# The opening of a linear-attention and state-space block: k of chunks 0 and 1 interleaved by passes, the first loads in four other parts

## The chip, the cores and the metric

The kernel runs on one core of a Trainium2 chip. The metric is the device time of one execution in microseconds (us), lower is better. Before the change the median of three runs is 179.42 us (178.81 to 181.05).

The engines are named as in the profile: PE is TensorE, which multiplies matrices, and PEld its weight loads; DVE is VectorE, ACT is ScalarE, POOL is GpSimd, SP is SyncE, which here issues all DMA transfers. Each engine works through its own queue in order and waits for the others by semaphores.

## The reference

One block mixes two branches of the same input x (2048 x 448):

```
qkv  = x @ wqkv                      # 448 -> 3 x 448, 16 heads of 28
phi  = lambda t: where(t > 0, t + 1, exp(t)) + 1e-6
kv   = sum over s of phi(k)[s] outer v[s], per head;   z = sum over s of phi(k)[s]
a    = (phi(q) @ kv / (phi(q) . z + 1e-6)) @ wo          # linear attention, not causal
b    = irfft(rfft(x) * rfft(K)) + x * D_skip             # long convolution, K from the state-space parameters
g    = sigmoid(sum(x * gate_w))
out  = g * a + (1 - g) * b
```

All is in 32-bit floats, and the kernel must keep that accuracy.

## The kernel before

**Tiling.** The 2048 rows of x are 16 chunks of 128 (`NC`). The width 448 is contracted in four blocks (`J`): three of 128 and block 0, which holds the last 64 columns. Each x chunk comes twice from memory: turned (`turned[c]`, 128 x 512, the four blocks side by side, used as weights of TensorE) and plain (`plain[c]`).

**Two halves of each number.** TensorE multiplies in the type fp32r, which keeps fewer bits. So each operand is split: the high half is a copy into fp32r (done by ScalarE, or VectorE), the low half is the original minus the high half (`low`, line 228). A product is then three: high x high, low x high and high x low. In `pieces` (line 307) these are the lists `hh`, `lh` and `hl`, one entry per block. Block 0 has only 64 columns; its other 64 rows hold the same x again against the low half of the weights, so `hl` lacks block 0, and a projection of one chunk is **eleven** matmuls (4 + 4 + 3) into one PSUM tile. I write h1 for the product of high halves of block 1, l1 for x low by weights high, w1 for x high by weights low; where loads, copies and low halves are spoken of, w1 is the weight block 1 itself.

**The order is written out by hand.** The scheduling is manual: every engine's queue has its instructions in the order of the program, and only the waits are put in by the framework. So the order of the lines from 419 on is the order of each queue.

**The opening** (lines 180 to 252 and 419 to 460):

- Before the data are there, `fill(WARM)` (line 252) issues nine bf16 matmuls of a tile of ones into a PSUM tile that nobody reads.
- SP issues the first loads in the three parts of `PARTS` (lines 30 and 200 to 209): part 1 is x of chunk 0 and block 1 of the k weights (256 + 224 KB), part 2 is weight blocks 2 and 3 (448 KB), part 3 weight block 0 and x of chunk 1 (224 + 256 KB). Behind them come two transfers of 512 KB (x of chunk 2 turned, and the plain x of chunks 0 to 2), the q weights (two of 450 KB), the skip row (224 KB) and x of chunk 3 (line 219, `load_x`).
- VectorE copies the high half of chunk 0's x in two pieces (420, 422), and subtracts the low halves of x and of each weight block (423 to 426); ScalarE copies the high halves of the weight blocks 1, 2, 3, 0 (421 and 256).
- `pieces(0, ..., "k", "w")` (427) orders the eleven products of chunk 0 as h1 l1 h2 l2 w1 h3 l3 w2 w3 h0 l0; they are issued in groups with three more filling matmuls between (428 to 430).
- `split_t(1)` (432) copies chunk 1's x to its high half on ScalarE and subtracts the low half on POOL; then `project(1, ...)` issues chunk 1's k, all eleven in a row, into the PSUM tile `v0`. Chunk 2 follows in the same way into `v1`.
- `k_feature`, `k_high` and `k_low` (346 to 361) make phi(k): two passes on ScalarE, one on VectorE, then `pkh` on ScalarE and `pkl` on VectorE. `zb` sums phi(k) on VectorE. `split_n(c)` splits plain x into `xn`: high on ScalarE, low on POOL.
- `do_g(c)` (384) adds x^T phi(k) of the chunk to four PSUM tiles that stay for the whole kernel: eleven matmuls, of which the first takes `pkh`, the second `pkl`, the third the low half of `xn`.
- The q weights are split (`split_w(..., wqh, ...)`, 445 to 448), and `project(0, wqh, ...)` (452) makes q of chunk 0, with block 0 last.

After that the 16 chunks go through q, k, the state update and the skip branch in a steady order until about 119 us; then the accumulated state is turned into small matrices, and the last 16 rounds (`attend`) make the output.

Of the kernel before, what the change touches and what calls it, by code (L numbers as in the profile page):

```python
# [8 lines left out]
F32R = mybir.dt.float32r  # L9
# [6 lines left out]
P = 128  # L16
S = 2048
D = 448
# [6 lines left out]
NAT = 4 * P  # L25
LO = NAT + D
XC = LO + 64
NX = XC - NAT + D
WARM = 9
PARTS = ((("x", 0), ("w", 1)), (("w", 2), ("w", 3)), (("w", 0), ("x", 1)))  # L30
FIRST = 2 * NAT + J * D
QA = 1
QW = D + 16
# [100 lines left out]
def gated_mix_kernel(ctx: ExitStack, tc: tile.TileContext, xin, wq_d, wvo_d, abc_d, ldt_d, dsk_d,  # L134
                     turn_d, cst_d, first_d, gin_d, lag_d, out):
    nc = tc.nc
    PE, ACT, DVE, POOL, SP = nc.tensor, nc.scalar, nc.vector, nc.gpsimd, nc.sync
# [15 lines left out]
    wkh, wkl = wk2[:, 0], wk2[:, 1]  # L153
# [21 lines left out]
    xt_p = work.enter_context(tc.tile_pool(name="xt", bufs=4))  # L175
# [11 lines left out]
    xt, xn, turned, plain = {}, {}, {}, {}  # L187
# [11 lines left out]
    o = 0  # L199
    for part in PARTS:  # L200
        e = o
# [7 lines left out]
        o = e  # L209
# [17 lines left out]
    def low(eng, o, r, h):  # L227
        eng.tensor_tensor(out=o, in0=r, in1=h.bitcast(F32), op=ALU.subtract)  # L228

    def split_t(c):  # L230
        w = xt[c] = xt_p.tile([P, 2 * NAT], F32R, name="xt", tag="t")
        ACT.copy(w[:, :NAT], turned[c])  # L232
        low(POOL, w[:, NAT:], turned[c], w[:, :NAT])

    def split_n(c):
        r, w = plain[c], xn_p.tile([P, NX], F32R, name="xn", tag="n")
        xn[c] = w
        ACT.copy(w[:, :XC - NAT], r)  # L238
        low(POOL, w[:, XC - NAT:], r[:, :D], w[:, :D])
        if c > 2:  # L240
            skip(c)

    def skip(c):
        POOL.tensor_tensor(out=y[:, c], in0=plain[c][:, :D], in1=dsk, op=ALU.mult)  # L244
# [3 lines left out]
    def fill(n):  # L248
        for _ in range(n):
            PE.matmul(idle, lhsT=warm[:, :P], rhs=warm, start=True, stop=True)  # L250

    fill(WARM)
    ACT.activation(oks, warm[:DJ, :1], AF.Exp)

    def split_w(j, h, l, w, eng):
        ACT.copy(h[:, j], w[j] if isinstance(w, dict) else w[:, j])
        low_w(j, h, l, w, eng)

    def low_w(j, h, l, w, eng):
        r = slice(0 if j else 64, P)  # L260
        w = w[j] if isinstance(w, dict) else w[:, j]
        low(eng, (l if j else h)[r, j], w[r], h[r, j])
# [44 lines left out]
    def pieces(c, wh, wl, n, tag, last=None):  # L307
        o = ps.tile([P, 512], F32, name=tag, tag=tag)
        h, l = ([xt[c][:, i + k * P:i + (k + 1) * P] for k in range(J)] for i in (0, NAT))
        hh, lh, hl = ([(a[k], w[:, k]) for k in range(J)] for a, w in ((h, wh), (l, wh), (h, wl)))  # L310
        hl = hl[1:]
        if last == "x":
            seq = hh + hl + lh
        else:
            seq = [p for k in range(J) for p in (hh[k], lh[k])] + hl
            if last == "w":
                seq = seq[2:6] + seq[8:9] + seq[6:8] + seq[9:] + seq[:2]

        def run(count):
            for _ in range(min(count, len(seq))):  # L320
                a, b = seq.pop(0)
                run.n += 1
                PE.matmul(o[:, :n], lhsT=a, rhs=b, start=run.n == 1, stop=not seq)  # L323
        run.n = 0
        return o, run

    def project(*args, **kw):
        o, run = pieces(*args, **kw)
        run(11)
        return o  # L330
# [15 lines left out]
    def k_feature(c, o):  # L346
        e = tp.tile([P, D], F32, name="e", tag="e")
        pks[c] = o[:, :D]
        ACT.activation(e, pks[c], AF.Relu, scale=-1.0)  # L349
        ACT.activation(e, e, AF.Exp, scale=-1.0)  # L350
        DVE.scalar_tensor_tensor(out=pks[c], in0=pks[c], scalar=1.0, in1=e, op0=ALU.add, op1=ALU.max)  # L351

    def k_high(c):
        pkh[c] = tp.tile([P, D], F32R, name="pkh", tag="pkh")
        ACT.add(pkh[c], pks[c], 1e-6)

    def k_low(c):
        pk = pks.pop(c)
        pkl[c] = tp.tile([P, D], F32R, name="pkl", tag="pkl")
        for o, a, op in ((pkl[c], pkh[c].bitcast(F32), ALU.subtract), (zb, zb, ALU.add))[::-1 if c == NC - 1 else 1]:  # L360
            DVE.scalar_tensor_tensor(out=o, in0=pk, scalar=1e-6, in1=a, op0=ALU.add, op1=op)
# [54 lines left out]
        for _ in range(n):  # L416
            next(prep, None)

    w = xt[0] = xt_p.tile([P, 2 * NAT], F32R, name="xt", tag="t")
    DVE.tensor_copy(w[:, P:NAT], turned[0][:, P:])  # L420
    ACT.copy(wkh[:, 1], wkr[1])  # L421
    DVE.tensor_copy(w[:, :P], turned[0][:, :P])
    low(DVE, w[:, NAT:], turned[0], w[:, :NAT])
    low_w(1, wkh, wkl, wkr, DVE)
    for j in (2, 3, 0):
        split_w(j, wkh, wkl, wkr, DVE)
    ko, run = pieces(0, wkh, wkl, D, "k", "w")
    for n, f in ((1, 1), (1, 1), (6, 0), (1, 1), (2, 0)):
        run(n)
        fill(f)  # L430
    ko = [ko]
    split_t(1)
    ko.append(project(1, wkh, wkl, D, "v0", "x"))
    split_t(2)
    ko.append(project(2, wkh, wkl, D, "v1", "x"))
    k_feature(0, ko[0])
    k_high(0)
    split_n(0)
    k_low(0)
    k_feature(1, ko[1])  # L440
    split_n(1)
# [20 lines left out]
    for c in range(2, NC - 2):  # L462
# [7 lines left out]
        ko = project(c + 1, wkh, wkl, D, "v1" if c in (2, 4) else "k")  # L470
# [39 lines left out]
        for j in {11: (0, 1), 12: (2, 3)}.get(c, ()):  # L510
            w = xn_p.tile([P, NX], F32R, name="wo", tag="n")[:DJ, :2 * D].rearrange("p (i d) -> p i d", i=2)
# [113 lines left out]
    c = NC - 2  # L625
    POOL.memset(rows[DT:RX, D:2 * D], 0.0)
    gate(0, c)
    ko = project(c + 1, wkh, wkl, D, "k")
# [31 lines left out]
    gates_c(NC - 2, g[0], "pkl")()  # L660
    norm_b(1)
    qo, q_run = pieces(c + 1, wqh, wql, D + 2, "q")
    for i in range(5):
        phi(i)
# [170 lines left out]
def _layout(inputs):  # L835
# [15 lines left out]
    def tiles(w):  # L851
        o = np.zeros((P, J, w.shape[1]), np.float32)
        for k in range(3):
            o[:, k + 1] = w[k * P:(k + 1) * P]
        o[:64, 0] = w[384:]
        o[64:, 0] = w[384:]
        return o
# [8 lines left out]
                          for n in ("B_log_A_real", "B_A_imag", "B_C_real", "B_C_imag")]  # L866
                         + [np.repeat(np.asarray(inputs["B_log_dt"]).reshape(D, 1, 1), P, axis=1),
                            x[:, ::-1].transpose(2, 1, 0)], axis=2)
    wk = tiles(w[:, D:2 * D])
    first = np.concatenate([wk[:, i] if kind == "w" else xin[i, :, :NAT] for part in PARTS for kind, i in part]  # L870
                           + [xin[2, :, :NAT], xin[0, :, NAT:], xin[1, :, NAT:], xin[2, :, NAT:]], axis=1)
# [42 lines left out]
```

## Time and profile before

| | us |
|---|---|
| median of three runs | 179.42 |
| lowest and highest run | 178.81, 181.05 |
| the profiled execution | 178.89 |
| its span in the trace | 177.1 |
| PE busy | 170.5 |
| ACT busy | 96.2 |
| DVE busy | 113.4 |
| POOL busy | 121.1 |

The profile is of one execution. Its span runs from the first to the last recorded instruction; 1.79 us lie around it. Rows of the timeline read: start, length, engine, line of the kernel, operation, output <- inputs, shape, count, and in brackets how long the engine stood idle before and what ended that. A row with a count over 1 covers several instructions in a row, from the first start to the last end. Rows of the chain that ended last read: start, length, engine, tile and line.

### The profile page before, as it was taken

The page shows a single profiled execution, that of the slowest core. Times are in us where ns is not written, and L with a number is a line of the kernel's source. Part 1 is how long each engine was busy: PE and PEld are TensorE (multiplying, and loading weights), DVE is VectorE, ACT ScalarE, POOL GpSimd, SP SyncE. Part 2 cuts the span into 40 slices and gives each one's busy share as a digit, 9 for nine tenths or more (in the row PEclk, how much of TensorE's full clock was granted, in tenths as well). Part 3 has the DMA queues.
Part 4 walks back from the last instruction along what each step waited for, and adds up shares of the span by engine and source line. Part 5 has one row for each costly group of instructions (what it writes and reads, how often), then busy time and mean ns, then how long its engine had stood idle before and what let it go on. Part 6 is the DMA issues. An engine that isn't in the chain of part 4 may idle for free.

```text
span 177.1 us, 2803 instructions
## 1 busy us (share of the span) xinstructions
PE 170.5 (96%) x876; PEld 151.6 (86%) x876; DVE 113.4 (64%) x244; ACT 96.2 (54%) x220; POOL 121.1 (68%) x128
## 2 busy tenths in 40 slices
PE   6999999999999999999999999999889999999991
PEld 2699999999999999999989999988678999999991
DVE  1747538698857274462824619376999988977451
ACT  3789388874536244272435753464645555564541
POOL 5167476977349969688599999439089999893100
PEclk9999999999999999999999999999999999999999
DMA  5999973095003303032133000000121212222313
GB/s 174 414 316 269 249 223 127 8 418 227 4 1 120 106 16 119 5 120 75 45 121 123 0 0 1 0 2 5 21 47 52 105 74 86 104 75 82 111 55 104
DMA packets 7963, 18.61 MB, mean 105 GB/s; under 512 B 2045, under 2 KB 4810, under 8 KB 7818
## 3 DMA queue, kind: packets, MB, share of 16 engines
q1 hardware_dynamic: 7946, 18.41, 31.6%
q8 instruction: 7, 0.11, 0.3%
q14 instruction: 10, 0.08, 0.2%
HBM read 14.38 MB, written 3.67 MB: 102 GB/s over the span
## 4 chain that ended last, share of the span: by engine, by line
PE 91%; DVE 4%; DMA 2%; ACT 1%; issue 0%; DVEq 0%; ACTq 0%
PE a L612 21%; PE g L392 20%; PE q L323 18%; PE k L323 16%; PE v L323 6%; PE tr L587 3%; DMA y<-in 2%; PE v L400 2%; PE v L399 2%; PE k L706 1%; DVE kvl L228 1%; DVE wk L694 1%; PE m L686 0%; DVE rc L677 0%; PE q L250 0%; DVE den L530 0%
## 5 line engine op out<-in xcount | busy, mean ns | idle before, releaser
L612 PE MATMUL a<-wk,th 128*128 128x448 f32 (+1 forms) x170 | 36.9, 363 | 0.7 <-DVE wk L694 0.7
L392 PE MATMUL g<-pkh,xn 128*128 128x448 f32 x112 | 35.6, 366 | 0.0
L612 PEld LDWEIGHTS a<-wk,th 128*128 128x128 f32 x170 | 29.5, 189 | 2.9 <-DVE wk L694 0.9
L323 PE MATMUL k<-wk,xt 128*128 128x448 f32 x132 | 29.6, 368 | 0.2 <-ACT wk L421 0.2
L351 DVE SCALAR_TENSOR_TENSOR k<-k,e 128x448 f32<-128x448 f32 x12 | 7.6, 632 | 32.1 <-ACT e L350 32.1
L323 PE MATMUL q<-wqh,xt 128*128 128x450 f32 x120 | 28.0, 370 | 0.0
L323 PEld LDWEIGHTS k<-wk,xt 128*128 128x128 f32 x132 | 24.6, 188 | 3.1 <-ACT wk L421 0.7
L412 POOL TENSOR_TENSOR y<-y,t 128x448 f32<-128x448 f32 x16 | 18.8, 1175 | 12.3 <-DVE t L404 11.9
L228 POOL TENSOR_TENSOR xn<-xr,xn 128x448 fp32r<-128x448 f32 x16 | 19.3, 1203 | 9.2 <-ACT xn L238 9.0
L323 PEld LDWEIGHTS q<-wqh,xt 128*128 128x128 f32 x120 | 22.5, 189 | 2.2 <-issue 0.2
L392 PE MATMUL g<-pkl,xn 128*128 128x448 f32 x64 | 23.4, 366 | 0.0
L392 PEld LDWEIGHTS g<-pkh,xn 128*128 128x128 f32 x112 | 21.0, 188 | 2.5
L349 ACT ACTIVATE e<-k 128x448 f32<-128x448 f32 x12 | 6.5, 546 | 28.0 <-PE k L323 27.9
L525 POOL TENSOR_TENSOR prod<-pq,zb 128x448 f32<-128x448 f32 x16 | 18.4, 1159 | 4.3 <-ACT zb L647 3.1
L244 POOL TENSOR_TENSOR y<-xr,rows 128x448 f32<-128x448 f32 x16 | 18.9, 1184 | 0.0
L228 POOL TENSOR_TENSOR xt<-xr,xt 128x512 fp32r<-128x512 f32 x14 | 18.2, 1299 | 0.4 <-ACT xt L232 0.4
L550 POOL TENSOR_TENSOR pn<-pq,den 128x336 f32<-128x336 f32 x16 | 12.1, 754 | 8.3 <-DVE den L539 4.4
L617 DVE SCALAR_TENSOR_TENSOR ot<-y,og,a 128x448 f32<-128x448 f32 (+1 forms) x17 | 10.6, 626 | 5.6 <-PE a L612 5.5
L595 DVE TENSOR_TENSOR th<-tr,th 128x512 fp32r<-128x512 f32 x16 | 11.0, 690 | 3.0 <-ACT th L594 2.5
L594 ACT CAST th<-tr 128x512 fp32r<-128x512 f32 x16 | 9.4, 590 | 5.5 <-PE tr L587 5.3
L392 PEld LDWEIGHTS g<-pkl,xn 128*128 128x128 f32 x64 | 11.2, 175 | 1.0
L323 PE MATMUL q<-wql,xt 128*128 128x450 f32 x45 | 11.7, 364 | 0.0
(149 smaller groups left out, 301.6 us busy)
## 6 DMA issues: line engine op xcount, KB each, us to landing
xr<-in SPq DMA_DIRECT2D x15, 512.0 KB, 6.0
out<-ot SPq DMA_DIRECT2D x15, 224.0 KB, 2.0
pq<-in SPq DMA_DIRECT2D x4, 448.0 KB
wvo<-in SPq DMA_DIRECT2D x1, 1792.0 KB
y<-in SPq DMA_DIRECT2D x2, 480.0 KB
y<-in SPq DMA_DIRECT2D x2, 450.0 KB
u<-t SPq DMA_DIRECT2D x30, 1.8 KB, 1.8
y<-in SPq DMA_DIRECT2D x1, 448.0 KB, 4.4
```

The source lines that it names most:

```text
L228: eng.tensor_tensor(out=o, in0=r, in1=h.bitcast(F32), op=ALU.subtract)
L244: POOL.tensor_tensor(out=y[:, c], in0=plain[c][:, :D], in1=dsk, op=ALU.mult)
L323: PE.matmul(o[:, :n], lhsT=a, rhs=b, start=run.n == 1, stop=not seq)
L351: DVE.scalar_tensor_tensor(out=pks[c], in0=pks[c], scalar=1.0, in1=e, op0=ALU.add, op1=ALU.max)
L392: PE.matmul(g[i][:a.shape[1], :D], lhsT=a, rhs=b, start=c == 0 and n == 0, stop=c == NC - 1 and n == len(seq) - 1)
L412: POOL.tensor_tensor(out=y[:, c], in0=y[:, c], in1=t, op=ALU.add)
L525: POOL.tensor_tensor(out=pd[c], in0=pq[:, c], in1=zb, op=ALU.mult)
L550: POOL.tensor_tensor(out=n[:, :3, :DJ].rearrange("p j (h d) -> p j h d", h=4), in0=a, in1=r[:, :H - 4].rearrange("p (j h) -> p j h", j=3)[ ...
L594: ACT.copy(h, ov)
L595: DVE.tensor_tensor(out=l, in0=ov, in1=h.bitcast(F32), op=ALU.subtract)
L612: PE.matmul(a[:, lo:hi], lhsT=u_, rhs=w_[:, lo:hi], start=n == 0, stop=n == 10)
L617: DVE.scalar_tensor_tensor(out=ot[:, lo:hi], in0=y[:, c, lo:hi], scalar=og[:, c:c + 1], in1=a[:, lo:hi], op0=ALU.mult, op1=ALU.add)
```

## The change

Three things change in the opening, and nothing behind `k_low(0)`.

1. The first loads come in four parts: x of chunks 0 and 1 (512 KB), weight block 1 (224 KB), weight blocks 2 and 3 (448 KB), weight block 0 (224 KB). The same bytes, one transfer more.
2. The 22 products of k of chunks 0 and 1 are interleaved in an order written out as a string per chunk. The three filling matmuls between them go; one is added ahead (`WARM` 10). In order, with c0 and c1 for the chunks: c0 h1, c1 h1, c0 l1, c0 w1, c1 w1, c0 h2, c1 h2, c0 l2, c0 h3, c1 l1, c1 h3, c0 w2, c0 l3, c0 w3, c1 l2, c1 w2, c1 l3, c0 h0, c0 l0, c1 w3, c1 h0, c1 l0.
3. The high half of chunk 1's x is copied by ScalarE ahead of weight block 1, and its low half is subtracted by VectorE, behind the low half of weight block 1, instead of by POOL. `split_n(0)` stands ahead of `k_high(0)` instead of behind it.

```diff
-WARM = 9
-PARTS = ((("x", 0), ("w", 1)), (("w", 2), ("w", 3)), (("w", 0), ("x", 1)))
+WARM = 10
+PARTS = ((("x", 0), ("x", 1)), (("w", 1),), (("w", 2), ("w", 3)), (("w", 0),))
...
-            if last == "w":
+            if last and len(last) > 1:
+                seq = [{"h": hh, "l": lh, "w": [None] + hl}[i[0]][int(i[1])] for i in last.split()]
+            elif last == "w":
                 seq = seq[2:6] + seq[8:9] + seq[6:8] + seq[9:] + seq[:2]
...
-    w = xt[0] = xt_p.tile([P, 2 * NAT], F32R, name="xt", tag="t")
+    w, w1 = (xt_p.tile([P, 2 * NAT], F32R, name="xt", tag="t") for _ in range(2))
+    xt[0], xt[1] = w, w1
     DVE.tensor_copy(w[:, P:NAT], turned[0][:, P:])
+    ACT.copy(w1[:, :NAT], turned[1])
+    DVE.tensor_copy(w[:, :P], turned[0][:, :P])
     ACT.copy(wkh[:, 1], wkr[1])
-    DVE.tensor_copy(w[:, :P], turned[0][:, :P])
     low(DVE, w[:, NAT:], turned[0], w[:, :NAT])
     low_w(1, wkh, wkl, wkr, DVE)
+    low(DVE, w1[:, NAT:], turned[1], w1[:, :NAT])
     for j in (2, 3, 0):
         split_w(j, wkh, wkl, wkr, DVE)
-    ko, run = pieces(0, wkh, wkl, D, "k", "w")
-    for n, f in ((1, 1), (1, 1), (6, 0), (1, 1), (2, 0)):
-        run(n)
-        fill(f)
-    ko = [ko]
-    split_t(1)
-    ko.append(project(1, wkh, wkl, D, "v0", "x"))
+    ko, runs = zip(*(pieces(c, wkh, wkl, D, t, o) for c, t, o in (
+        (0, "k", "h1 l1 w1 h2 l2 h3 w2 l3 w3 h0 l0"), (1, "v0", "h1 w1 h2 l1 h3 l2 w2 l3 w3 h0 l0"))))
+    for c, n in ((0, 1), (1, 1), (0, 2), (1, 1), (0, 1), (1, 1), (0, 2), (1, 2), (0, 3), (1, 3), (0, 2), (1, 3)):
+        runs[c](n)
+    ko = list(ko)
     split_t(2)
     ko.append(project(2, wkh, wkl, D, "v1", "x"))
     k_feature(0, ko[0])
+    split_n(0)
     k_high(0)
-    split_n(0)
     k_low(0)
```

## The prediction

> **What bounds the kernel now.** I read the page first (share of each engine), then the chain that ended last, then the rows of the first 20 us engine by engine, because the change touches nothing later than the first output of chunk 1.
>
> ```profile
> span 177.1 us, 2803 instructions
> PE 170.5 (96%) x876; PEld 151.6 (86%) x876; DVE 113.4 (64%) x244; ACT 96.2 (54%) x220; POOL 121.1 (68%) x128
> ```
>
> TensorE is busy nearly all the time, so time is gained only where it stands still, or lost where a new wait makes it stand still. The profiled execution took 178.89 us, 1.79 us more than its span, and lies 0.53 us under the median of 179.42 us.
>
> ```profile
> 0.76 3.81 DMA y<-in
> 4.59 0.57 ACT wk L421
> 5.21 0.47 PE k L323
> 5.91 0.43 PE k L323
> 6.57 1.43 PE k L323 x7
> 8.23 0.59 PE k L323 x2
> 8.82 4.48 PE v L323 x22
> 13.30 4.46 PE g L392 x22
> ```
>
> Columns: start, length, what. The opening is a load (to 4.59), a copy on ScalarE, and then matmuls. One matmul of the dense stretch takes 4.48/22 = 0.204 us. The eleven of chunk 0's k come in four pieces with gaps; the 22 of chunks 1 and 2 (`v`) and the 22 of both first state updates (`g`) come without.
>
> ```profile
> 13.13 0.37 PE L392 MATMUL g<-pkh,xn 128*128 128x448 f32 x1
> 13.34 0.36 PE L392 MATMUL g<-pkl,xn 128*128 128x448 f32 x1
> 15.57 0.36 PE L392 MATMUL g<-pkl,xn 128*128 128x448 f32 x1
> 17.59 0.99 PE L323 MATMUL q<-wqh,xt 128*128 128x450 f32 x4
> ```
>
> From the first matmul (5.21) to the first of the state update (13.13) pass 7.92 us; 33 matmuls at 0.204 need 6.72. So **1.20 us** is all that dense interleaving can win there. After 17.6 only the shift counts: the chain of waits shows TensorE dense behind it.
>
> **The first matmul moves back.** Today the first part carries x of chunk 0 and w1 (480 KB), the second w2 and w3 (448), the third w0 and x of chunk 1 (480).
>
> ```profile
> 0.76 1.35 SPq L208 DMA_DIRECT2D y<-in  x3
> 4.59 0.56 ACT L421 CAST wk<-y 128x448 fp32r<-128x448 f32 x1 [2.34 <-DMA y<-in]
> 5.67 0.57 ACT L256 CAST wk<-y 128x448 fp32r<-128x448 f32 x1 [0.52 <-DMA y<-in]
> 6.87 0.57 ACT L256 CAST wk<-y 128x448 fp32r<-128x448 f32 x1 [0.16 <-DMA y<-in]
> 4.68 0.53 SPq L192 DMA_DIRECT2D xr<-in  x1
> ```
>
> ScalarE waits for each part and starts at 4.59, 5.67 and 6.87, that is after 480, 928 and 1408 KB: 415 and 400 KB per us, with no fixed cost between parts. On this line the new parts come at 4.67 (both x, 512 KB), 5.21 (w1, 736 KB), 6.31 (w2 and w3, 1184 KB), 6.87 (w0, 1408 KB). A fourth issue costs SP 1.35/3 = 0.45 us, still over by 2.6, long before its data are due. SP's later loads move by one place: the ninth issue (4.68 today, just as the first part is in) becomes the tenth and goes out at about 5.2, but the transfers ahead of it (1408 KB of parts, two of 512 KB, 900 KB of q weights, 224 KB) take more than 8 us at that rate, so the queue is full beyond 11 us and nothing lands later for it.
>
> w1's landing is not in this trace. It lies between 4.67 (together with x) and 5.67 (the start after 928 KB); I take 5.21, by bytes. The Trainium skill, "DMA: Bandwidth & Descriptors", section on the anatomy of one DMA, gives each transfer a fixed 2.0 us besides its bytes, measured on the software path: read as a cost per part in sequence, that would put w1 about 2 us later, and the sum at some 2 us slower. The 1.08 us from the first to the second part contradict it for queued transfers: the fixed part overlaps.
>
> On ScalarE the high half of chunk 1's x now stands first.
>
> ```profile
> 11.16 0.61 ACT L238 CAST xn<-xr 128x512 fp32r<-128x512 f32 x1
> 11.67 0.55 ACT L349 ACTIVATE e<-v 128x448 f32<-128x448 f32 x1
> ```
>
> A 512-wide copy blocks ScalarE for 0.51 us, so it runs from 4.67 and frees the engine at 5.18: w1's copy then waits for its load and ends at 5.21 + 0.56 = 5.77; the first matmul follows 0.06 later, as now (4.59 + 0.56 to 5.21), at **5.83**, 0.62 us later than before. The copies of w2, w3, w0 end at 6.87, 7.35 and 7.82.
>
> **VectorE's queue** has one 512-wide subtraction more (POOL has it now, with time to spare).
>
> ```profile
> 4.59 0.36 DVE L420 CAST xt<-y 128x384 fp32r<-128x384 f32 x1 [3.17 <-DMA y<-in]
> 4.87 0.22 DVE L422 CAST xt<-y 128x128 fp32r<-128x128 f32 x1
> 5.12 0.69 DVE L228 TENSOR_TENSOR xt<-y,xt 128x512 fp32r<-128x512 f32 x1
> 5.73 0.62 DVE L228 TENSOR_TENSOR wk<-y,wk 128x448 fp32r<-128x448 f32 x1
> 6.27 0.63 DVE L228 TENSOR_TENSOR wk<-y,wk 128x448 fp32r<-128x448 f32 x1
> ```
>
> Spacing is 0.61 us behind a 512-wide one and 0.54 behind a 448-wide one. So chunk 0's low half ends at 5.89, w1's at 6.43, chunk 1's at 7.04 (0.61 of delay for those behind it), w2's at 7.58, w3's at 8.12, w0's at 8.67.
>
> **The 22 interleaved matmuls**, each at the later of 0.204 behind the last one and 0.06 behind its operand. c0 h1 5.83, c1 h1 6.03, c0 l1 6.24; c0 w1 waits for w1's low half, 6.49 instead of 6.44; c1 w1 6.69; c0 h2 waits for w2's copy, 6.93 instead of 6.90; then c1 h2, c0 l2 at 7.13 and 7.34. From there nothing is late: h3 stands at 7.54 (copy 7.35), c1 l1 at 7.74 (7.04), c0 w2 at 8.15 (7.58), c0 w3 at 8.56 (8.12), c0 h0 at 9.37 (8.67). The last of chunk 0 (the nineteenth) starts at 9.57, the last of chunk 1 at 10.18, chunk 2's k at 10.39, and the state update could start at **12.63**, 0.50 before today's 13.13. So 1.20 us of gaps become 0.08, and 0.62 is paid for the later start.
>
> **What is late next.** k of chunk 0 is finished later, though k of chunk 1 is earlier than it need be.
>
> ```profile
> 8.86 0.55 ACT L349 ACTIVATE e<-k 128x448 f32<-128x448 f32 x1
> 9.44 0.58 ACT L350 ACTIVATE e<-e 128x448 f32<-128x448 f32 x1
> 10.05 0.63 DVE L351 SCALAR_TENSOR_TENSOR k<-k,e 128x448 f32<-128x448 f32 x1 [1.96 <-ACT e L350]
> 10.72 0.55 ACT L355 ACTIVATE pkh<-k 128x448 fp32r<-128x448 f32 x1 [0.70 <-DVE k L351]
> 11.30 0.62 DVE L361 SCALAR_TENSOR_TENSOR pkl<-k,pkh 128x448 fp32r<-128x448 f32 x1 [0.61 <-ACT pkh L355]
> 11.84 0.62 DVE L361 SCALAR_TENSOR_TENSOR zb<-k,zb 128x448 f32<-128x448 f32 x1
> 11.85 1.16 POOL L228 TENSOR_TENSOR xn<-xr,xn 128x448 fp32r<-128x448 f32 x1 [1.27 <-ACT xn L238]
> ```
>
> This serial chain from the end of k to `pkl` takes 11.92 - 8.86 = 3.06 us. Today it ends 1.4 us before its use at 13.34. After the change k ends at 9.57 + 0.37 = 9.94, the chain starts at 9.99, `pkh` is there at 12.41 and `pkl` at 13.05. The state update's first matmul goes at 12.63, but its second must wait to **13.11** where TensorE would be ready at 12.83: 0.28 us lost, a new wait. The moved `split_n(0)` costs nothing: the copy of xn now runs in ScalarE's 0.70 us of idling before `pkh` and POOL's low half ends at about 12.9, before its use at 13.31; with the old order it would end at about 14.1.
>
> Chunk 1: ScalarE starts its relu 0.44 behind `pkh` of chunk 0 (10.72 to 11.16), 12.30; exp 12.88 to 13.46; VectorE is free of `zb` at 13.52; its max ends at 14.15, `pkh` at 14.73, `pkl` at 15.39. Its matmul, 2.23 behind that of chunk 0 as today (13.34 to 15.57), would go at 15.34 and waits to **15.45**: 0.12 us before 15.57. Behind ScalarE's delayed `pkh` (some 0.65 us) are the four copies of the q weights.
>
> ```profile
> 15.49 1.49 ACT L256 CAST wqh<-y 128x450 fp32r<-128x450 f32 x3
> 16.59 1.02 POOL L228 TENSOR_TENSOR wql<-y,wqh 128x450 fp32r<-128x450 f32 x1 [1.00 <-ACT wqh L256]
> 17.01 1.08 DVE L228 TENSOR_TENSOR wqh<-y,wqh 64x450 fp32r<-64x450 f32 x1 [0.24 <-ACT wqh L256]
> ```
>
> All shift by about 0.65: w0's last row ends at 18.75. The q projection, at 17.59 - 0.12 = 17.47, takes the w0 products last, from 9 x 0.204 behind, 19.31. It is covered with 0.55 us to spare; past that, each us of delay would cost a us. Chunk 2's feature and chunk 3's x are used from 22 us on.
>
> **Sum**: +0.62 (start) - 1.12 (gaps) + 0.28 (`pkl` of chunk 0) + 0.11 (of chunk 1), about -0.1 us. Against its own execution that is 178.8, against the median 179.42 - 0.1 = **179.3 us**. The three fills left out cost nothing if the clock holds.
>
> **Rivals.**
>
> *TensorE goes back to the slow clock (slower).*
>
> ```profile
> PEclk9999999999999999999999999999999999999999
> 1.48 3.55 PE L250 MATMUL q<-warm 128*128 128x512 bf16 x9 [1.48 <-DVE warm L181]
> 4.01 0.15 PEld L250 LDWEIGHTS <-warm 128*128 128x128 bf16 x1 [0.28 <-issue]
> 4.43 0.10 PEld L250 LDWEIGHTS <-warm 128*128 128x128 bf16 x1 [0.27 <-issue]
> ```
>
> The granted clock is full in every slice, so the slow start shows only in durations: the fills first run at 0.42 us each (4.01 to 4.43), and weight loads go from 0.15 to 0.10 after 2.95 us of work. Ten fills end near 5.25; then TensorE stands for 0.58 us, against 0.18 today, and no fill bridges the small waits. Were it to fall back, 448 columns would take 0.42 x 448/512 = 0.37 us, for another 2.95 us until the clock is back: (1 - 0.204/0.37) x 2.95 = 1.3 us, so 180.6 us. It decides when the idle stretch before the first matmul is enough to drop the clock. For it: the fills stand in today's gaps. Against: right behind today's gaps the chain's seven k matmuls from 6.57 take 0.204 us each, at full speed, and after the change TensorE is dense from 6.9 on. The Trainium skill, "TensorE: Matmul & The Clock Gate", Part 1, has the clock fall only after an idle window of about 3.4 us; by that rule 0.58 us does nothing. Chance 0.06.
>
> *w1 lands later (a little slower).* Every 0.1 us of its landing goes through `pkl` of both chunks to the end one for one, since both waits hang on the first matmul; from 5.33 on the kernel is slower. At 5.67, the upper bound, it is 0.34 us slower: 179.8 us. For it: more and shorter rows in the queue. Against: 400 to 415 KB per us at both steps of today. Chance 0.22.
>
> *The new waits on `pkl` don't come (faster).* If the chain of chunk 0 is shorter than 3.06 us, or the first matmul earlier (w1 in with x: ScalarE's two copies then end at 5.74), the gaps are saved whole: 0.5 us, 178.9 us. Against: every row of that chain follows its predecessor within 0.05 us. Chance 0.12.
>
> *The loads or the order don't do what they say*: the time stays at 179.4 us, 0.05; not to be told from the forecast by time.
>
> **How the numbers follow.** The forecast (within 0.2 us of 179.3) has 0.55. The bounds of the landing and of the `pkl` waits give 178.9 to 179.8. Runs of the same kernel lay between 178.81 and 181.05 us, 0.6 below the median and 1.6 above it; with most of that below, a part of it above and a share of the clock's rival the range is **178.3 to 180.5**. A change of 2%, about what a measurement of this kernel can tell from no change, is 3.6 us: three times the gaps that there are to win, and more than the clock's rival costs. So faster 0.01, same 0.96, slower 0.03.
>
> **What the profile after would show.** Right: first k matmul near 5.83; two `k`/`v` rows alternating without gaps over 0.1 us; chunk 2's k from 10.4; a wait of about 0.3 us for `pkl` in the first state update and of 0.1 in the second; first q matmul near 17.47; chunk 1's low half on VectorE and none on POOL. Wrong: weight loads of 0.3 us or more after 5.8 (the clock), w1's copy later than 5.3 (the load), a wait before h2 or h0 of the q projection (ScalarE's queue), or the k chain over 3.1 us.

## The result

The changed kernel takes 180.24 us (median of 20 runs, 179.85 to 182.95) against 179.09 us before (20 runs, 178.75 to 181.05): **0.69% slower**, ratio 1.0069 (95% interval 1.0040 to 1.0098). The forecast was 179.3 us, 0.1 us faster than the 179.42 us that three runs of the kernel before had given. The time lies inside the range, but on the other side of no change. The executions of both kernels fall into two groups some 1.6 us apart, with 4 of 20 before and 9 of 20 after in the upper one, so that one time alone says little.

The page of the changed kernel (compare the first two lines shown of before):

```profile
span 178.3 us, 2800 instructions
PE 170.9 (96%) x874; PEld 151.8 (85%) x874; DVE 114.0 (64%) x245; ACT 96.2 (54%) x220; POOL 120.0 (67%) x127
```

The profiled execution took 180.12 us, 1.23 us more than the one of before, and the span grew by 1.2 us. Where, the chain that ended last tells. Its rows of after (start, length, what):

```profile
1.47 4.45 PE q L250 x10
13.46 4.59 PE g L394 x21
18.05 2.25 PE q L325 x11
...
169.04 4.70 PE a L615 x33
...
173.77 0.46 DVE ot L620
```

and the end of the same chain in the kernel before:

```profile
168.76 4.70 PE a L612 x33
...
173.49 0.46 DVE ot L617
...
174.02 0.35 ACT pq L623
```

The first q projection stands at 18.05 (17.76 before), the last matmuls at 169.04 (168.76), the last work on VectorE at 173.77 (173.49). So the opening costs 0.28 us, it is carried unchanged through 150 us, and **0.9 us of the 1.2 arise behind the last work of any engine**. I call the stretch from the end of ScalarE's last copy to the end of the span the tail: 177.1 - 174.37 = 2.7 us before; after, from this row of the timeline,

```profile
174.30 0.34 ACT L626 COPY pq<-a 128x224 f32<-128x224 f32 x1 [0.88 <-DVE ot L620]
```

178.3 - 174.64 = 3.7 us (2.69 and 3.64 by the unrounded times of the traces, which are used below). No engine records work in it. What the DMA view shows in it are the last data of the output and two loads of instructions. In the kernel before, both lie in one window, 175.8 to 176.0 us (columns: queue, kind, packets, MB, share of the engines):

```profile
q14 instruction: 2, 0.02, 24.6%
```

In the changed kernel one lies in 176.0 to 176.2 and the other in 177.2 to 177.4:

```profile
q14 instruction: 1, 0.01, 10.1%
...
q14 instruction: 1, 0.01, 16.8%
```

The first comes 1.5 us behind the last copy in both kernels, and the end follows about 1.1 us behind the second in both. The second has moved by 1 us. What SP does meanwhile is shown below, with the experiments on the place of the transfers.

The opening of after, from TensorE's and ScalarE's timelines:

```profile
4.50 0.62 ACT L424 CAST xt<-y 128x512 fp32r<-128x512 f32 x1 [2.25 <-DMA y<-in]
4.86 0.15 PEld L250 LDWEIGHTS <-warm 128*128 128x128 bf16 x1 [0.28 <-issue]
5.08 0.56 ACT L426 CAST wk<-y 128x448 fp32r<-128x448 f32 x1
5.69 0.28 PEld L325 LDWEIGHTS k<-wk,xt 128*128 128x128 f32 x1 [0.68 <-ACT wk L426]
5.69 0.74 PE L325 MATMUL k<-wk,xt 128*128 128x448 f32 x1
5.86 0.33 PEld L325 LDWEIGHTS v<-wk,xt 128*128 128x128 f32 x1
6.23 0.57 PE L325 MATMUL v<-wk,xt 128*128 128x448 f32 x1
6.61 0.65 PE L325 MATMUL k<-wk,xt 128*128 128x448 f32 x2
7.09 0.37 PE L325 MATMUL v<-wk,xt 128*128 128x448 f32 x1
7.29 0.37 PE L325 MATMUL k<-wk,xt 128*128 128x448 f32 x1
7.50 0.57 ACT L256 CAST wk<-y 128x448 fp32r<-128x448 f32 x1 [0.28 <-DMA y<-in]
8.75 0.62 ACT L232 CAST xt<-xr 128x512 fp32r<-128x512 f32 x1 [0.68 <-DMA xr<-in]
9.74 0.57 PE L325 MATMUL k<-wk,xt 128*128 128x448 f32 x2
10.15 3.02 PE L325 MATMUL v<-wk,xt 128*128 128x448 f32 x14
13.01 0.36 PE L394 MATMUL g<-pkh,xn 128*128 128x448 f32 x1
13.46 0.47 PE L394 MATMUL g<-pkl,xn 128*128 128x448 f32 x1
15.78 0.45 PE L394 MATMUL g<-pkl,xn 128*128 128x448 f32 x1
17.89 0.98 PE L325 MATMUL q<-wqh,xt 128*128 128x450 f32 x4
```

Weight loads of 0.28 and 0.33 us and matmuls 0.38 us apart (6.23 to 6.61) mean the slow clock; from 7.1 us on they are 0.19 and 0.20 us. The trace records one step of the clock to full speed, at 6.8 us here and at 4.4 us in the profile of before. From 7.1 us on the matmuls are dense.

### The profile page after: what moved, and what is told of

It reads as the page before. It is cut to its first block, busy times and chain, and to the rows that moved or that the text cites. A ratio compares the mean times of both kernels' runs of the same rounds, so it can differ in the third digit from the quotient of the medians.

```text
span 178.3 us, 2800 instructions
## 1 busy us (share of the span) xinstructions
PE 170.9 (96%) x874; PEld 151.8 (85%) x874; DVE 114.0 (64%) x245; ACT 96.2 (54%) x220; POOL 120.0 (67%) x127
## 4 chain that ended last, share of the span: by engine, by line
PE 91%; DVE 5%; ACT 2%; issue 1%; DVEq 0%; ACTq 0%
PE a L615 20%; PE g L394 20%; PE q L325 18%; PE k L325 15%; PE v L325 5%; PE tr L590 3%; PE q L250 2%; PE v L402 2%; PE v L401 2%; PE k L709 1%; DVE kvl L228 1%; DVE wk L697 1%; PE m L689 0%; DVE rc L680 0%; DVE k L353 0%
## 5 line engine op out<-in xcount | busy, mean ns | idle before, releaser
L325 PEld LDWEIGHTS k<-wk,xt 128*128 128x128 f32 x132 | 25.1, 190 | 2.8 <-ACT wk L426 0.7
```

## Experiments

All kernels are compared with the kernel before in the same session. Two questions: what makes the tail, and what the opening is worth by itself.

### Whose instructions make the tail

The change makes SP's program one transfer longer (226 instructions for 225), VectorE's one instruction longer, POOL's one operation shorter, and TensorE's two filling matmuls shorter. Four kernels do one of these each to the kernel before.

One transfer more on SP:

```diff
-    SP.dma_start(out=both, in_=turn_d)
+    for i in range(2):
+        SP.dma_start(out=both[:, i], in_=turn_d[:, i])
```

> The kernel before, with the load of `both` issued as two transfers instead of one, so SP's stream is one transfer longer as in the change, and nothing else differs. The profile of the change ends its last copy only 0.27 us later than before (174.64 against 174.37) but its span 1.2 us later: the stretch from the last copy to the end of the span (below: the tail) is 3.66 against 2.73 us. Theory 1 (the tail depends on the position of each engine's instructions in its stream, and it is SP's that matters): tail 3.6, time +0.9 us. If it is another engine's: tail 2.7 and no change. Theory 2 (the tail of the profiled run after the change is chance, and the slow opening is the whole cause): tail 2.7, no change.

Measured: ratio 1.0111 (1.0060 to 1.0163), from four runs between 179.62 and 181.95 us, so that the size of the loss is uncertain. The tail is not: the last copy ends at 174.22, 0.15 earlier than before, and the span is 177.8: tail 3.6 us.

```profile
core 0 of [0], span 177.8 us
...
173.87 0.35 ACT L624 COPY pq<-a 128x224 f32<-128x224 f32 x1 [0.88 <-DVE ot L618]
```

One instruction more on VectorE:

```diff
     DVE.memset(warm, 1.0)
+    DVE.memset(keep.tile([1, 8], F32, name="pad"), 0.0)
```

> The kernel before, with one more tiny memset (1x8) on VectorE at the start, where it idles for 3 us: VectorE's stream is one instruction longer, as in the change. Theory 1 with VectorE's stream: tail 3.6, time +0.9 us. With another engine's, or theory 2: tail 2.7 and no change.

Measured: 1.0007 (0.9978 to 1.0037), tail 2.7.

One less on POOL:

```diff
-    POOL.tensor_copy(ones, warm[:, :P])
+    DVE.tensor_copy(ones, warm[:, :P])
...
-    DVE.tensor_copy(w[:, P:NAT], turned[0][:, P:])
+    DVE.tensor_copy(w[:, :NAT], turned[0])
...
-    DVE.tensor_copy(w[:, :P], turned[0][:, :P])
```

> The kernel before, with the copy of `ones` on VectorE instead of POOL and VectorE's two copies of chunk 0's x in one: POOL's stream one instruction shorter, as in the change, VectorE's as long as before. Theory 1 with POOL's stream: tail 3.6, time +0.9 us. Otherwise tail 2.7 and at most 0.1 us slower (the longer copy ahead of the first matmul).

Measured: 1.0009 (0.9974 to 1.0043), tail 2.7.

The fills of the change:

```diff
-WARM = 9
+WARM = 10
...
-    for n, f in ((1, 1), (1, 1), (6, 0), (1, 1), (2, 0)):
+    for n, f in ((1, 0), (1, 0), (6, 0), (1, 0), (2, 0)):
```

> The kernel before, with ten filling matmuls ahead and none between the pieces of chunk 0's k, as in the change: TensorE's stream is as much shorter. Theory 1 with TensorE's stream: tail 3.6, time +0.9 us. Rival (the fills keep the clock up): slow weight loads (0.28 us or more) between 5.2 and 9 us and up to 1 us more. Neither: no change, as the tenth fill ends before the first matmul can start.

Measured: 0.9982 (0.9953 to 1.0012), tail 2.7. So the one transfer alone gives the whole tail, VectorE, POOL and TensorE give none, and the fills between the pieces of k were worth nothing measurable. The other way round, the changed kernel with a transfer less:

```diff
-    for j in range(0, J, 2):
-        SP.dma_start(out=wqr[:, j:j + 2], in_=wq_d[:, j:j + 2])
+    SP.dma_start(out=wqr, in_=wq_d)
```

> The changed kernel, with the two loads of the q weights issued as one, so SP's stream is as long as before (225 instructions, 226 in the change and in the first experiment); all else as changed. Theory 1 (the tail goes with the length of SP's stream): tail 2.7 us, and what is left is the opening alone: 179.0 to 179.4 us, ratio 0.998 to 1.002. Rival (several streams count, or the change itself makes the tail): tail 3.6, 180.2 us.

Measured: **1.0005 (0.9988 to 1.0021)**, 179.26 against 179.17 us.

```profile
core 0 of [0], span 177.2 us
...
174.16 0.35 ACT L625 COPY pq<-a 128x224 f32<-128x224 f32 x1 [0.88 <-DVE ot L619]
```

The tail is 2.7 us again, and no loss is left that these runs can tell. A control for this edit, on the kernel before:

> The kernel before, with the two loads of the q weights issued as one: one transfer fewer than before. A control for the edit that took the tail away in the changed kernel: if the edit itself does nothing, tail 2.7 and 179.1 us; if a shorter stream of SP gains more, a shorter tail.

Measured: 0.9998 (0.9960 to 1.0036), tail 2.8: by itself the edit changes the time by nothing that these runs can tell.

### Instructions, number of transfers, or their place

One, then eight instructions more on SP that move no data:

```diff
+    for _ in range(8):
+        SP.drain()
     SP.dma_start(out=both, in_=turn_d)
```

> The kernel before, with one SP instruction more that moves no data (a drain ahead of the load of `both`): 226 instructions, as many transfers as before. Theory 1a (the position in SP's stream): tail 3.6 us, time +0.9. Theory 1b (the number of transfers, their rings or semaphores): tail 2.7, no change.

> The kernel before, with eight SP instructions more that move no data. One of them did not lengthen the tail, one transfer more did. Theory 1a (position in SP's stream, of which a transfer takes several places): tail 3.6, time +0.9. Theory 1b (the number of transfers): tail 2.7, no change.

Measured: 0.9991 (0.9975 to 1.0007) with one and 0.9993 (0.9954 to 1.0032) with eight, tails 2.7 and 2.7. The length of SP's program isn't it. My first theory fell with these.

Each transfer reports its end on one of eight semaphores, which the transfers take in turn. I number them 0 to 7 in the order of the first eight transfers. By the records of the traces the last three transfers that ran stand on 5, 6, 7 in the kernel before and on 6, 7, 0 in the changed one. (The expectations below count one place too low. I had read their numbers in the listing of SP's program, at waits that belong to a part that the kernel jumps over.)

Three runs tell number from place. The load of `both` is cut into two pieces on the changed kernel, and into nine or three on the kernel before.

> The changed kernel with the load of `both` issued as two: one transfer more again, so two more than before. The transfers take eight semaphores in turn; at the end SP waits for those of the last three, which are number 4, 5, 6 before, 5, 6, 7 after the change and 6, 7, 0 here. Theory 1c (the tail depends on where in the turn of eight the last transfer stands, 7 being the bad place): tail 2.7 us and 179.3 us, so one more transfer makes the changed kernel 0.9 us faster. Theory 1d (each count from one more on, by the length of SP's stream): tail 3.6 or more, 180.2 us.

> The kernel before, with the load of `both` in nine pieces: eight transfers more, so the last ones stand on semaphores 4, 5, 6 as before, while SP's stream is eight instructions longer. Theory 1c (place in the turn of eight): tail 2.7 us, no change. Theory 1d (length of SP's stream): tail 3.6, +0.9 us.

> The kernel before, with the load of `both` in three pieces: two transfers more, the last on semaphores 6, 7, 0. Theory 1c: tail 2.7 us, unless number 0 is a bad place too. Theory 1d: tail 3.6 us.

With the earlier runs, in order of the number of transfers:

| kernel | transfers that ran | places of the last three | tail, us | time against before |
|---|---|---|---|---|
| before, q weights in one load | 95 | 4, 5, 6 | 2.78 | 0.9998 |
| before | 96 | 5, 6, 7 | 2.69 | 1 |
| after, q weights in one load | 96 | 5, 6, 7 | 2.67 | 1.0005 |
| after | 97 | 6, 7, 0 | 3.64 | 1.0069 |
| before, one transfer more | 97 | 6, 7, 0 | 3.63 | 1.0111 |
| after, one transfer more | 98 | 7, 0, 1 | 3.56 | 1.0065 (1.0048 to 1.0081), four runs |
| before, two more | 98 | 7, 0, 1 | 3.55 | 180.0 us, one run |
| before, eight more | 104 | 5, 6, 7 | 2.67 | 1.0015 (0.9989 to 1.0041) |

The last row carries the verdict: eight transfers more, and the tail is short again. (The profiled execution of that kernel took 180.52 us, 1.5 us more than the median of its ten runs, and its last copy ends late; its tail is read from it, its time from all ten.)

```profile
core 0 of [0], span 178.7 us
...
175.70 0.34 ACT L627 COPY pq<-a 128x224 f32<-128x224 f32 x1 [0.88 <-DVE ot L621]
```

So neither length nor number decides, but **where in the turn of eight the last transfer falls**. I had expected one bad place alone, and there are at least two: as the last place only 6, 7, 0 and 1 were tried.

Why the place matters stands in the traces. Behind the last transfer SP takes eight waits, one for each semaphore, in all sixteen traces in the order 0 to 7. Waits don't count as work, so the timeline leaves them out, but the trace records when SP passed each. In us behind the end of the last copy:

| kernel (place of the last transfer) | last data landed | waits 0, 1, 2, 3, 4, 5, 6, 7 passed at | tail |
|---|---|---|---|
| before (7) | 1.27 | 0.16, 0.27, 0.36, 0.44, 0.52, 0.94, 1.03, 1.28 | 2.69 |
| before, q weights in one load (6) | 1.25 | 0.16, 0.27, 0.36, 0.44, 0.52, 0.59, 1.26, 1.36 | 2.78 |
| after, one transfer more (1) | 1.28 | 0.16, 1.30, 1.40, 1.81, 1.91, 2.00, 2.07, 2.15 | 3.56 |
| after (0) | 1.25 | 1.27, 1.37, 1.47, 1.54, 1.96, 2.06, 2.14, 2.22 | 3.64 |

The last data land 1.24 to 1.28 us behind the last copy in all sixteen traces, and the span ends about 1.4 us behind the last of the eight waits. With the last transfer on 7, SP passes the seven other waits while the data are still on their way. With it on 0, SP stands at the first wait until they have landed and passes the other seven only then: the eighth comes at 2.22 instead of 1.28 us, and these 0.94 us are all but 0.01 of what the tail grew by. The view of what SP waited for (in all, times, longest) from 170 us on shows the same, before and then after (the eight waits carry the number of the line at which the kernel jumps over its second half, 824 and 827):

```profile
SPq L824 <- SPq L824: 0.8, 3, 0.4
```

```profile
SPq L827 <- SPq L827: 1.7, 2, 1.3
```

Within the eight waits there is a pause of 0.42 us (0.52 to 0.94 before, 1.54 to 1.96 after). Before, it is covered by the flight of the data; what causes it no run shows. The second load of instructions comes some 0.3 us behind the last of the eight waits in both kernels (1.57 behind 1.28, 2.59 behind 2.22), so it can't have held them up. The Trainium skill, "Runtime: NRT & Kernel Launch", section on instruction fetch, says that a taken branch out of the buffered instructions forces a load before execution goes on. The two loads in the tail, where the kernel jumps past its second half, agree with that; no run shows which engine waits for them.

### What the parts of the opening are worth

With the tail taken away, each part can be undone or moved in the changed kernel (q weights in one load, 179.26 us). `split_n(0)` back behind `k_high(0)`:

```diff
-    split_n(0)
     k_high(0)
+    split_n(0)
```

> The changed kernel with SP's stream as before (q weights in one load), and with `split_n(0)` behind `k_high(0)` again. By the prediction's working the low half of chunk 0's xn would end some 1.2 us later, at about 14.4, and the third matmul of the state update would wait for it to about 14.5 instead of 13.8: 0.7 us later, of which the next chunk's wait takes back at most 0.2. So +0.5 to +0.7 us against the kernel with the new order. Rival (the order makes no difference, because other waits cover it): within 0.1 us.

Measured: 180.11 us, 1.0051 (1.0031 to 1.0071), 0.85 us slower than with the new order.

```profile
7.37 0.47 PE L324 MATMUL k<-wk,xt 128*128 128x448 f32 x1 [0.31 <-ACT wk L255]
...
14.71 0.67 PE L393 MATMUL g<-pkh,xn 128*128 128x448 f32 x2 [0.55 <-POOL xn L227]
...
18.94 0.99 PE L324 MATMUL q<-wqh,xt 128*128 128x450 f32 x4
```

The third product of the state update now waits 0.55 us for POOL's low half of xn, as worked out. (The wait at 7.37 is a load of weight blocks 2 and 3 that came some 0.4 us later in this execution; it is not the edit's.)

The low half of chunk 1's x back on POOL:

```diff
-    low(DVE, w1[:, NAT:], turned[1], w1[:, :NAT])
+    low(POOL, w1[:, NAT:], turned[1], w1[:, :NAT])
```

> The changed kernel with SP's stream as before, and the low half of chunk 1's x subtracted on POOL again, early. POOL takes 1.29 us from about 5.15, so it is there at 6.5, before its first use near 8.1, and VectorE's three later subtractions come 0.6 us earlier; nothing waits for any of them in the profile after. So no difference to the kernel with it on VectorE, within 0.1 us. Rival (VectorE's queue holds the interleaved matmuls up): up to 0.4 us faster.

Measured: 179.94 us, 1.0045 (1.0032 to 1.0058), 0.7 us slower. Both theories missed.

```profile
5.40 1.67 POOL L227 TENSOR_TENSOR xt<-y,xt 128x512 fp32r<-128x512 f32 x1 [2.30 <-ACT xt L423]
...
5.86 1.69 DVE L227 TENSOR_TENSOR wk<-y,wk 128x448 fp32r<-128x448 f32 x1
...
7.61 0.47 PE L324 MATMUL k<-wk,xt 128*128 128x448 f32 x1 [0.81 <-DVE wk L227]
```

VectorE's subtraction for weight block 1 takes 1.69 us instead of 0.63: it begins while POOL's runs and ends 0.48 us after POOL's end at 7.07; POOL's own took 1.67 instead of 1.29. TensorE waits 0.81 us for it. The Trainium skill, "SBUF — State Buffer", section "Who interferes with whom", says that a VectorE instruction with two inputs in SBUF and a POOL instruction that reads SBUF need the same pair of ports, which one of them holds for its whole length while the other stands; the trace agrees. The same pair of rows was there in the profile of before, at 17.01 us: VectorE's subtraction of 1.08 us that ends 0.48 us after POOL's of 16.59 to 17.61. So the move of this subtraction to VectorE, which I costed as a delay of 0.61 us that nothing waits for, is what keeps the interleaving from being slower.

The last two products of chunk 0 three places earlier:

```diff
-(0, 3), (1, 3), (0, 2), (1, 3)):
+(0, 3), (0, 2), (1, 3), (1, 3)):
```

> The changed kernel with SP's stream as before (q weights in one load), and the last two products of chunk 0 (h0, l0) issued three places earlier, ahead of l2, w2 and l3 of chunk 1. The theory of the new wait: the gain of the opening is lost because k of chunk 0 ends late and its chain of 3.06 us to `pkl` holds the state update up (0.25 us over what TensorE needs, and 0.1 in the second). Three places are 0.61 us, so both waits go: 0.3 to 0.45 us faster than without this edit (179.26 us), 178.8 to 179.0. Rival (the clock or something else sets the time, the waits are covered): no difference.

Measured: 178.79 us, 0.9968 (0.9935 to 1.0001). TensorE's rows, first of the changed kernel with the short tail, then of this one:

```profile
12.85 0.36 PE L393 MATMUL g<-pkh,xn 128*128 128x448 f32 x1
13.30 0.47 PE L393 MATMUL g<-pkl,xn 128*128 128x448 f32 x1
...
15.62 0.45 PE L393 MATMUL g<-pkl,xn 128*128 128x448 f32 x1
...
17.73 0.98 PE L324 MATMUL q<-wqh,xt 128*128 128x450 f32 x4
```

```profile
5.94 0.47 PE L324 MATMUL k<-wk,xt 128*128 128x448 f32 x1 [0.40 <-ACT wk L425]
...
7.11 0.45 PE L324 MATMUL k<-wk,xt 128*128 128x448 f32 x1
...
12.91 0.36 PE L393 MATMUL g<-pkh,xn 128*128 128x448 f32 x1
13.12 0.37 PE L393 MATMUL g<-pkl,xn 128*128 128x448 f32 x1
...
15.38 0.37 PE L393 MATMUL g<-pkl,xn 128*128 128x448 f32 x1
...
17.45 0.99 PE L324 MATMUL q<-wqh,xt 128*128 128x450 f32 x4
```

Both waits for `pkl` are gone (0.21 us between first and second product instead of 0.45), and q starts 0.28 us earlier although the first matmul was 0.2 us later in this execution. It was timed in another session than the kernel without the edit. It is the fastest of all kernels by its median; its interval just reaches 1, so that it beats the kernel before is likely and not shown.

## Why the prediction was wrong

**The step that failed is the extra transfer costed at nothing.** I followed the fourth transfer through SP's queue (0.45 us of issue, later loads one place back, nothing lands later). That holds for TensorE, which waits for no load behind w1. But two loads did land later: weight block 0 at 7.50 instead of the 6.87 forecast, and x of chunk 2 at 8.75 instead of 8.15 before. What failed is that I took what lies behind the last work as a constant of the kernel, both the 1.79 us outside the span and the stretch inside it, and asked of the transfer only who needs its data. The same transfer moved the last one of the program from the semaphore that SP waits for last to the one that it waits for first, and the tail went from 2.69 to 3.64 us. Without it the changed kernel is 1.0005 of before. No rival named it, and the sentence that only the shift counts after 17.6 us is wrong by 0.9 us. That the time still lies inside the range is luck: the range was made wide for the spread of the runs and for the clock, not for this.

**The opening** was forecast at -0.12 us and reads +0.30 in the profile (17.89 for 17.59); over all runs it is +0.1 us (-0.2 to +0.4) by the kernel with the short tail, which can't be told from either.

- *First matmul* 5.83 forecast, 5.69 measured. Both loads came early in this execution: x was there at 4.50 instead of 4.67, and w1 by 5.08 instead of 5.21, as ScalarE went from x straight to w1 without a wait. The rival of a late w1 is out for this execution.
- *Interleaving*: c0 h2 was to start at 6.93 and starts at 7.29. Counted from the first matmul it is 1.60 us instead of 1.10. Most of that is the clock, the term that I set at zero: full speed came at 6.8 us, in the middle of the first matmuls. In the execution with chunk 0's last products earlier it came at 5.0 us, and the same six products take 1.17 us (5.94 to 7.11). I had that as a rival, but wrongly told: TensorE did not fall back for want of fills, it had not come up yet. In the profile of before the step lay at 4.4 us; I read that one execution as if it were the kernel's. The same ten fills, with the kernel before, made no difference.
- *Behind it* each term fits: from c0 h2 on all is 0.33 to 0.42 us later than forecast, and dense. The last product of chunk 0 starts near 9.94 (9.57); the chain from there to `pkl` takes 3.05 us (3.06); the wait in the first state update is 0.25 us (0.28) and in the second 0.1 (0.12); q starts at 17.89 (17.47).
- *The new wait on `pkl`* is confirmed by the rows of the order that takes it away: from the first product of the state update to q pass 4.54 us (12.91 to 17.45) instead of 4.88 (13.01 to 17.89), 0.34 less where 0.39 were forecast. The times go the same way, 0.5 us between the medians of the two kernels and 0.35 against their own sessions' before, but their intervals overlap.
- *`split_n(0)` moved costs nothing* is right, and it is needed: undone, 0.85 us are lost (0.5 to 0.7 expected).
- *The low half on VectorE*: its delay of 0.61 us was right (6.22, then 6.82), its worth was missed: on POOL it would have cost 0.7 us by holding VectorE up.
- *The fills* were worth nothing, as costed.

## What to carry over

A change at the start of a program can cost at its end: look at the stretch behind the last work in every comparison, and when it moves, see which semaphore the last transfer reports on and in what order the program waits for them. Here the last transfer should stand on the one that is waited for last. Interleaving moves the end of the first consumer's input back: give the tile that starts a long serial chain its last products first. Before moving an elementwise instruction with two inputs to POOL or VectorE, see what the other runs at that moment.

## What the runs showed of the hardware

- SP passes its eight waits at the end of the program one behind the other, mostly 0.07 to 0.11 us apart, also where their transfers have long landed. The tail is 2.67 to 2.69 us in the eleven kernels whose last transfer is on the eighth semaphore, 2.78 on the seventh (one kernel), 3.55 and 3.56 on the second, 3.63 and 3.64 on the first.
- The step to the full clock came at 4.2 to 6.9 us in the profiled executions, with the fills always beginning at 1.5 us. Where it came at 4.4 us, the 3.4 us ahead of it were filled for 2.9 us; where it came at 6.8 us, the window that ended 3.4 us earlier had been filled for 1.9 us. The traces' steps up and down lie 170.67 or 174.08 us apart, 50 or 51 times 3.413 us. The Trainium skill, "TensorE: Matmul & The Clock Gate", Part 1, has a free-running window of 3.4 us; these numbers agree with it, and put what counts as busy between 2.0 and 2.7 us of it (with the step at 4.2 us, a window filled for 2.7 us brought it; with the step at 6.9 us, the window before had been filled for 2.0 us and did not).
- The rows of the granted clock stand at full speed through those slow starts; only the durations of weight loads and matmuls show them.
